# Last layer: GpSimd makes some of the shifted copies of VectorE's exponential, each issued beside a first step that reads PSUM; the planner's thresholds there set anew

## The chip, the cores and the metric

The kernel runs on one core of a Trainium2 chip. The core has five engines with instruction queues of their own: TensorE (PE; its weight loads are listed as PEld), VectorE (DVE), ScalarE (ACT), GpSimd (POOL) and SyncE (SP), which issues the DMAs. Each runs its queue in order, and they meet through semaphores. The metric is the device time of one execution in microseconds, as the median over runs.

## The reference

Four layers are added to a stream `x` of 2048 tokens by 512 features: A, B, A, B. Each normalizes its input, projects it to 32 heads of 16 features, attends, and projects back.

```python
# layer A (inside four segments of 512 tokens, causal, and a memory of the segments before)
logits = einsum(qs, ks) * scale + mask;  p = softmax(logits);  a_dot = p @ vs
a_mem = phi(qs) @ M / (phi(qs) @ z + 1e-06);  o = g * a_mem + (1 - g) * a_dot
M = M + phi(ks)^T @ vs;  z = z + sum(phi(ks))
# layer B (all 2048 tokens against all, no mask)
scores = einsum('bhqd,bhkd->bhqk', q, k) * Dh ** (-0.5)
o = einsum('bhqk,bhkd->bhqd', softmax(scores), v)
# x = x + A(ln(x)); x = x + B(ln(x)); x = x + A(ln(x)); x = x + B(ln(x))
```

A layer B needs 32 x 2048 x 2048 exponentials, 128 million, and a matmul on either side of them. The last layer is a B.

## The kernel before

**Tiles.** A head's scores are made in transposed blocks of 128 keys by 512 queries, one PSUM bank each (PSUM has 8 banks of 512 float32 columns). Heads are done in groups: one group is the heads of a 128-row chunk `c` with parity `e`, four heads at the row offsets 0, 32, 64, 96, against one segment of 512 queries. For such a group the queries are copied into a masked tile `qm` (line 1424). In layer 3 a group has up to 64 banks.

**Units.** The loop in `attention` takes unit after unit. A unit is two or three banks of scores: PE computes them (`qm` against keys `KB`), then one ACT instruction takes the exponential of all of them at once, from PSUM into the tile `pT` (line 1514, 128x1024 for two banks, 128x1536 for three). Two sets of three banks alternate, so PE fills one while ACT reads the other. Some units later PE multiplies `pT` with the values (17 columns: 16 features and a one for the sum) into an accumulator bank, four heads in four column quarters.

**The exponential on DVE.** A part of the banks goes another way, called `dx`. When `compose` finds room, a unit gives up its third bank (bank 2 or 4 of PSUM), or a spare bank is used, or both. DVE reads this bank in a first step (`dx_first`, line 1121): scale, add a constant and write as uint16, whose bits are those of a bfloat16 near the exponential. One bank makes a first step of 512 columns, two banks one of 1024. The bits alone are too rough, so the tile is shifted: `dx_shift` (line 1184) adds a small constant to the uint16 values, which makes another rough exponential with its error elsewhere, and so on in a chain of four (`EXP_D`), or of three with weighted values (`W_D`). Every member of the chain is multiplied with the values by PE and added up in the accumulator. A chain runs over one, two or four banks at once, so a shift is 512, 1024 or 2048 columns wide. It goes in place, or into another free space: the tiles `dxw`, and in the last layers tiles that are no longer needed, `KA`, `QA`, `VA`, `woA`, `phk`, `phq`, `KB`, `VB`, `xT`. In the profile shifts therefore read `xT<-phq`, `KB<-VB` and the like, and first steps `VB<-ps`.

**What sets the order.** Nothing is decided on the chip. A class `Sched` records each instruction with a planned end, from durations given with each call, and derives the semaphores from what is read and written. The `Builder` asks this plan what to issue next: a first step only if DVE's planned time is near enough to the start of the unit (`dx_room`); shifts when DVE has credit, or to fill the time until a bank is ready (`fill`); products of shifted tiles when their planned end has passed (`pv_some`). Thresholds of these questions are class constants, and the list `PIECES` sets them anew whenever ACT's planned time passes the next of some forty marks. Four chains (`CHAINS`) may be open at once, each a generator `task_dx`. `dx_now` holds the space and banks of an open chain, `dx_use` how many readers a space still has, `dxq` the products that wait to be issued.

GpSimd has three kinds of work: causal masks of layer A, ones in the values, and the query masks `qm` in layers B. SP issues loads, transposes and the output.

Of the kernel before, what the change touches and what calls it, by code (L numbers as in the profile page):

```python
# [5 lines left out]
ALU = mybir.AluOpType  # L6
# [3 lines left out]
D = 512  # L10
# [12 lines left out]
UNIT, DXB, ACC = (0, 4), 3, 7  # L23
# [55 lines left out]
class Sched:  # L79


    def __init__(self):
        self.ops = {e: [] for e in ENGS}
        self.t = {e: 0.0 for e in ENGS}
        self.tiles = []

        self.streams = []
# [7 lines left out]
    def estimate(self, op, ns, gap, tile):  # L95
# [17 lines left out]
        elif e == "sp":  # L113
            st = max(ready, self.t[e])
            self.t[e] = st + max(gap, 600)
            op.end = st + ns
        else:
# [5 lines left out]
    def add(self, eng, fn, reads=(), writes=(), deps=(), name="", banks=(), ns=300, gap=None, tile=None):  # L123
# [47 lines left out]
        self.estimate(op, ns, max(ns - 85, 60) if gap is None else gap, tile)  # L171
# [86 lines left out]
class Builder:  # L258
# [9 lines left out]
    DX_RES, CHAINS, ALT, ALTS, ALTA = 0, 4, 0, 3, (1, 1, 1, 1)  # L268
    ORDER = [[(-4.6, 7.7, 7.6, 0.9, -10), (3.8, -10.8, 0.4, 20, -10.8), (19, 59.6, 22, 59.8, 12), (31, 44.3, 46.9, 10.6, 0.2)],
             [(-1.5, -6.7, -5.8, 20.8, 1.2), (-5.2, -1.6, 28.5, 28, 7), (21, 35.0, 8.2, 30, 27.7), (21, 48.0, 37, 23.6, 12.2)]]  # L270
    PIECES = [(20.0, {'DXA_REST': 14, 'EVAC_ACT': -300, 'LOW': 32}),
              (60.0, {'AHEAD': 500, 'CR_W': 1900, 'DXA_REST': 10, 'EVAC_ACT': -300, 'LOW': 24, 'wide': True}),
              (100.0, {'AHEAD': 500, 'CR_W': 1900, 'DQ': 1900, 'EVAC_ACT': -300, 'wide': True}),
              (140.0, {'AHEAD': 300, 'CR_W': 1400, 'DQ': 2200, 'DX_T': 480, 'EVAC_ACT': 0}),
              (180.0, {'DMA_LATE': 300, 'DX_FIN': 2500, 'DX_T': 480, 'PE_B': 5, 'PE_LOW': 5}),
              (220.0, {'DMA_LATE': 600, 'DX_FIN': 2000, 'DX_T': 430, 'LOW': 16, 'PE_B': 4, 'PE_LOW': 6, 'PVN': 6}),
              (260.0, {'DX_RES': 2, 'HOR': 100, 'LOW': 24, 'NEAR_N': 200, 'PVN': 4}),
              (300.0, {'DX_RES': 2, 'HOR': 100, 'MARGIN': 700, 'NEAR_N': 200}),
              (340.0, {'DMA_LATE': 300, 'DQ': 1900, 'DX_RES': 2, 'FILLS': 1, 'HOR': 100, 'MARGIN': 700, 'NEAR_E': 80, 'NEAR_N': 200}),
              (380.0, {'DMA_LATE': 300, 'DMA_STEPS': 3, 'DQ': 2500, 'DX_RES': 2, 'DX_T': 330, 'FILLS': 1, 'HOR': 100, 'MARGIN': 700, 'NEAR_E': 0, 'NEAR_N': 200}),  # L280
              (420.0, {'DMA_LATE': 300, 'DMA_STEPS': 3, 'DQ': 2500, 'DX_RES': 2, 'DX_T': 330, 'FILLS': 1, 'HOR': 100, 'MARGIN': 700, 'NEAR': 6, 'NEAR_E': 0, 'NEAR_N': 200}),
# [1604 lines left out]
```

## Time and profile before

| | |
|---|---|
| median of 3 runs | 1772.88 us (1772.08 to 1774.62) |
| span of the profiled execution | 1772.3 us |
| ACT busy in it | 1729.2 us, 98% |
| DVE busy | 1521.1 us, 86% |
| PE busy | 1586.6 us, 90% |
| POOL busy | 287.2 us, 16% |

Busy time is the time in which at least one instruction of the engine ran; the rest is waiting. Line numbers are those of the kernel before. A group's row gives the line, engine, operation, output and input tile and shape, the count, then busy time in us and the mean of one in ns, and behind the second bar the idle time in front of them with what ended it. Because several lines are helpers (line 445 records every matmul), tiles tell more than lines. Two instructions that follow each other on DVE or ACT overlap a little in the record, the second starting before the first has ended.

### The profile page before, as it was taken

The numbers are of one execution on the slowest core, as the hardware profiler recorded it, in microseconds if no ns is written. First come the engines' busy times: TensorE is split into PE (matmuls) and PEld (weight loads), VectorE is DVE, ScalarE is ACT, GpSimd is POOL, SyncE is SP. The second block draws the span as 40 slices with busy tenths as digits, with TensorE's granted clock in tenths as the row PEclk, the third lists the DMA queues.
The fourth block names the chain that finished last, engine by engine and source line by source line (L and its number), as shares of the span: only waits on it lengthen the run. The fifth ranks groups of instructions, "written<-read, shape, count | busy, mean of one in ns | idle before, by whom it ended". The sixth has DMA issues, their size and how long they took to land.

```text
span 1772.3 us, 42500 instructions
## 1 busy us (share of the span) xinstructions
PE 1586.6 (90%) x17251; PEld 568.1 (32%) x17436; DVE 1521.1 (86%) x3001; ACT 1729.2 (98%) x1674; POOL 287.2 (16%) x656
## 2 busy tenths in 40 slices
PE   7889898889898989989989988988898898889988
PEld 4445454553224222233222332332222222222222
DVE  6677766589995999888999879768999999999997
ACT  7989998999999999999999999999999999999998
POOL 4622515110006000113000240141100000000000
PEclk9999998999999999999999999999999999999999
DMA  6021111000001000000000010110000000000000
GB/s 173 20 46 29 32 20 25 14 9 7 13 7 16 4 13 13 2 19 14 8 13 13 5 34 7 19 26 13 2 13 1 1 7 7 1 1 7 7 1 13
DMA packets 86180, 30.01 MB, mean 17 GB/s; under 512 B 78816, under 2 KB 85472, under 8 KB 85984
## 3 DMA queue, kind: packets, MB, share of 16 engines
q1 hardware_dynamic: 85984, 27.29, 7.6%
q8 instruction: 136, 2.23, 0.5%
q14 instruction: 60, 0.49, 0.1%
HBM read 6.30 MB, written 2.10 MB: 5 GB/s over the span
## 4 chain that ended last, share of the span: by engine, by line
ACT 52%; PE 22%; issue 17%; DVE 6%; POOL 2%; DMA 1%; SPq 0%; ACTq 0%; DVEq 0%; POOLq 0%
ACT pT L1514 51%; PE ps L445 22%; POOL pT L1529 2%; DVE QA L1121 1%; ACT amem L697 0%; DVE dxw L1184 0%; DVE dxw L1121 0%; DMA xT<-xn 0%; DVE rg L809 0%; DVE VB L1121 0%; DVE VB L480 0%; DVE KA L1646 0%; DVE VA L1184 0%; DVE ob L1628 0%; DVE phq L700 0%
## 5 line engine op out<-in xcount | busy, mean ns | idle before, releaser
L1514 ACT ACTIVATE pT<-ps 128x1024 bf16<-128x1024 f32 (+4 forms) x1623 | 1697.0, 1201 | 27.8 <-PE ps L445 21.0
L445 PE MATMUL ps<-qm,KB 32*128 32x512 bf16 x3584 | 517.8, 384 | 79.0 <-ACT pT L1514 67.3
L445 PE MATMUL ps<-pT,VB 128*17 128x512 bf16 x2221 | 377.7, 384 | 8.7 <-ACT pT L1514 3.7
L1529 POOL TENSOR_SCALAR_AFFINE_SELECT pT<-pT 128x256 bf16<-128x256 bf16 (+2 forms) x524 | 213.0, 418 | 548.4 <-ACT pT L1514 535.9
L445 PEld LDWEIGHTS ps<-qm,KB 32*128 32x128 bf16 x3584 | 131.6, 91 | 458.1 <-ACT pT L1514 355.1
L1424 POOL TENSOR_SCALAR qm<-QB,par 128x512 bf16<-128x512 bf16 x88 | 66.9, 763 | 848.7 <-PE ps L445 769.4
L445 PEld LDWEIGHTS ps<-pT,VB 128*17 128x17 bf16 x2221 | 88.1, 87 | 240.0 <-issue 202.5
L1121 DVE TENSOR_SCALAR dxw<-ps 128x512 uint16<-128x512 f32 (+1 forms) x212 | 145.4, 697 | 4.5 <-PE ps L445 3.6
L445 PE MATMUL ps<-qm,KA 32*128 32x384 bf16 (+3 forms) x1024 | 104.3, 307 | 26.0 <-ACT pT L1514 19.5
L1121 DVE TENSOR_SCALAR VA<-ps 128x512 uint16<-128x512 f32 (+1 forms) x172 | 121.4, 720 | 5.8 <-PE ps L445 4.7
L1184 DVE TENSOR_SCALAR dxw<-dxw 128x1024 uint16<-128x1024 uint16 (+1 forms) x302 | 121.0, 411 | 3.5 <-PE ps L445 1.7
L1121 DVE TENSOR_SCALAR QA<-ps 128x512 uint16<-128x512 f32 (+1 forms) x168 | 117.8, 716 | 4.9 <-PE ps L445 4.1
L445 PE MATMUL ps<-qm,QA 32*128 32x512 bf16 x512 | 103.6, 384 | 19.9 <-ACT pT L1514 18.6
L445 PE MATMUL ps<-VA,pT 128*128 128x51 bf16 (+1 forms) x2560 | 108.6, 188 | 14.1 <-POOL pT L1529 6.5
L445 PE MATMUL ps<-dxw,VW 128*17 128x512 bf16 x437 | 108.7, 381 | 0.2 <-DVE dxw L1184 0.2
L445 PEld LDWEIGHTS ps<-VA,pT 128*128 128x128 bf16 x2560 | 85.6, 97 | 63.8 <-POOL pT L1529 30.3
L1121 DVE TENSOR_SCALAR VB<-ps 128x512 uint16<-128x512 f32 (+1 forms) x117 | 92.1, 804 | 2.8 <-PE ps L445 2.1
L1121 DVE TENSOR_SCALAR KB<-ps 128x512 uint16<-128x512 f32 (+1 forms) x98 | 77.9, 808 | 2.5 <-PE ps L445 2.1
L445 PE MATMUL ps<-pT,VA 128*17 128x512 bf16 x386 | 76.7, 384 | 2.2 <-ACT pT L1514 1.8
L445 PE MATMUL ps<-dxw,VB 128*17 128x512 bf16 x256 | 74.1, 381 | 0.0
L445 PE MATMUL ps<-VB,pT 128*128 128x34 bf16 (+1 forms) x1788 | 69.4, 186 | 2.0 <-ACT pT L1514 1.1
L445 PE MATMUL ps<-xT,wB 128*128 128x512 bf16 x224 | 63.0, 393 | 5.8 <-issue 2.7
(292 smaller groups left out, 2408.1 us busy)
## 6 DMA issues: line engine op xcount, KB each, us to landing
out_dram<-x SPq DMA_DIRECT2D x8, 256.0 KB, 2.1
x<-in_A_x_dram SPq DMA_DIRECT2D x3, 512.0 KB, 5.1
wB<-in_B_wqkv_dram SPq DMA_DIRECT2D x1, 1536.0 KB, 11.7
xT<-xn SPq DMA_TRANSPOSE x60, 2.4
oT<-ob SPq DMA_TRANSPOSE x36, 2.4
x<-in_A_x_dram SPq DMA_DIRECT2D x4, 128.0 KB, 2.7
wA<-in_A_wq_dram SPq DMA_DIRECT2D x1, 512.0 KB, 5.1
wA<-in_A_wk_dram SPq DMA_DIRECT2D x1, 512.0 KB, 6.1
```

The lines of the kernel that those rows point to most:

```text
L445: self.sc.add("pe", lambda e: e.matmul(out, lhsT, rhs, start=start, stop=stop, skip_group_check=True), reads=reads, banks=[(bank, "w", all ...
L1121: self.sc.add("dve", lambda e: e.tensor_scalar(d, o, SCALE * LOG2E * 128, W_C if dxs[0][:3] in self.wt else EXP_C, op0=ALU.mult, op1=ALU.add),
L1184: self.op("dve", lambda e: e.tensor_scalar(o, w, d, None, op0=ALU.add), reads=self.b_dxw[b0][:len(ents)], writes=wr, ns=(295, 425, 560, 69 ...
L1424: self.op(eng, (lambda m, q, col: lambda e: e.tensor_scalar(m, q, col, 0.0, op0=ALU.mult, op1=ALU.add))(m, q, col), reads=[bq, self.b_par] ...
L1514: self.sc.add("act", (lambda dst, src: lambda e: e.activation(dst, src, ACT.Exp, scale=SCALE))(dst, src), writes=self.b_pT[slot * 3 + i:sl ...
L1529: self.op("pool", (lambda blk, pat: lambda e: e.affine_select(blk, blk, pattern=pat, compare_op=ALU.is_ge, fill=0.0, base=0, channel_multi ...
```

## The change

The class constant `PSH` switches the new part on. `PIECES` sets it to 2 at 1240 us of ACT's planned time, which is in the last layer, and `PSH_N` is 12, from 1720 us on 20. The rest of the new `PIECES` holds differences only, where the old one repeated values, and before 1240 it gives the same thresholds: both programs are identical up to there. From 1240 on the thresholds differ as well.

With `PSH` on, `dx_first` looks behind every first step whether GpSimd's planned time is early enough. If so, `pool_claim` picks an open chain whose next member can be made (or opens a waiting one), and `pool_part` issues a copy of as many banks as the first step has on GpSimd: the same addition of a constant on uint16. It waits for the DVE instruction in front of the first step (`self.sc.ops["dve"][-2]`), beside the semaphores that its data need. A shift of four banks thus becomes two to four copies. A claimed chain goes on when all its copies have been issued; what is left is issued at once in `task_dx`. In the plan, GpSimd and those DVE instructions that do not touch PSUM now exclude each other (`shared`).

```diff
+    def shared(self, eng, at, ns):
+        for e, a, b in self.held:
+            if e != eng and a <= at < b:
+                at = b
+        self.held = self.held[-5:] + [(eng, at, at + ns)]
+        return at
...
+        elif port and self.lock:
+            st = self.shared(e, max(self.t[e], ready), gap)
+            op.end = self.t[e] = max(st + gap, ready + ns)
...
+    PSH, PSH_N, DXP = 0, 12, 0
...
+              (1240.0, {'NEAR': 14, 'PVN': 3, 'PVHOLE': 250, 'DMA_LATE': 300, 'PSH': 2}),
+              (1280.0, {'NEAR': 10, 'DMA_LATE': 600}),
...
+              (1640.0, {'FILL_DVE': 0, 'DX_T': 480, 'DXA': 4, 'DX_WAIT': 200}),
...
+        if self.PSH and self.wide and max(self.sc.t["pool"], 0) <= self.sc.t["dve"] - (520, 1040)[k - 1]:
+            if not any(p and p["at"] < len(p["ents"]) for p in self.pooled):
+                self.pool_claim()
+            for p in self.pooled:
+                if p and p["at"] < len(p["ents"]):
+                    self.pool_part(p, k, self.sc.ops["dve"][-2])
+                    break
...
+    def pool_take(self, k, now):
+
+        b0, ents = now
+        g = ents[0][0]
+        j = self.dx_at[k] + 1 if self.dx_now[k] else 1
+        D = self.chords(ents)
+        if g is not self.cur and g not in self.sel or len(g.banks) - g.pos < self.PSH_N:
+            return False
+        b = b0 if self.dx_free(b0, len(ents)) or not self.dx_left(len(ents)) else self.dx_pick(len(ents))
...
+    def pool_part(self, job, n, sync):
+
+        b0, b, ents, i0 = job["b0"], job["b"], job["ents"], job["at"]
+        n = min(n, len(ents) - i0)
+        lo, hi = 512 * i0, 512 * (i0 + n)
+        w, o, d = self.dx_space(b0)[:, lo:hi], self.dx_space(b)[:, lo:hi], job["d"]
+        wr = [x for i in range(i0, i0 + n) for x in self.dx_writes(b, i)]
+        self.sc.add("pool", lambda e: e.tensor_scalar(o, w, d, None, op0=ALU.add), reads=self.b_dxw[b0][i0:i0 + n], writes=wr,
+                    deps=[sync] if sync is not None else [], ns=180 + 512 * n, gap=170 + 512 * n, name="dxp%d" % n)
```

What this does to the order, at three places. In the changed kernel lines have other numbers: 1134 is the first step, 1211 the shift, 1597 the exponential on ACT, 1507 the query mask, 1259 the new copy.

GpSimd's queue at the start of the last layer, before: the query masks and the ones in the values, and nothing more to the end.

```order
L1424 TENSOR_SCALAR qm<-QB,par 128x512 x4
L882 MEMSET VB 128x32 x3
L1424 TENSOR_SCALAR qm<-QB,par 128x512 x2
L882 MEMSET VB 128x32
L1424 TENSOR_SCALAR qm<-QB,par 128x512 x32
```

The same place of GpSimd's queue in the changed kernel:

```order
L1507 TENSOR_SCALAR qm<-QB,par 128x512 x6
L1259 TENSOR_SCALAR dxw<-dxw 128x512 x2
L1259 TENSOR_SCALAR QA<-dxw 128x512
L1507 TENSOR_SCALAR qm<-QB,par 128x512 x2
L1259 TENSOR_SCALAR QA<-dxw 128x512
L1259 TENSOR_SCALAR dxw<-phk 128x1024
L1507 TENSOR_SCALAR qm<-QB,par 128x512 x2
L1259 TENSOR_SCALAR dxw<-xT 128x512 x2
L1259 TENSOR_SCALAR woA<-KB 128x512 x2
L1259 TENSOR_SCALAR woA<-KB 128x1024
```

Copies now stand between the query masks: 200 of 512 and 54 of 1024 columns to the end of the program, with 26 masks among or behind them.

DVE's queue in the last layer behind the finish of the eighteenth group from the end (`x<-x,ps` adds the output projection to the stream), before:

```order
L1121 TENSOR_SCALAR VA<-ps 128x512 x2
L1184 TENSOR_SCALAR VB<-VB 128x2048
L1184 TENSOR_SCALAR VB<-VA 128x2048
L1184 TENSOR_SCALAR QA<-VB 128x2048
L1121 TENSOR_SCALAR KB<-ps 128x512
L911 TENSOR_TENSOR x<-x,ps 128x512
L1121 TENSOR_SCALAR KB<-ps 128x512 x2
L1184 TENSOR_SCALAR woA<-VB 128x2048
```

And in the changed kernel:

```order
L1134 TENSOR_SCALAR KA<-ps 128x512 x2
L1211 TENSOR_SCALAR xT<-KA 128x2048
L1134 TENSOR_SCALAR VB<-ps 128x512 x2
L924 TENSOR_TENSOR x<-x,ps 128x512
L1211 TENSOR_SCALAR VA<-xT 128x2048
L1134 TENSOR_SCALAR VB<-ps 128x512 x3
L1211 TENSOR_SCALAR QA<-VB 128x2048
L1134 TENSOR_SCALAR VB<-ps 128x512 x3
L1211 TENSOR_SCALAR phq<-VB 128x2048
```

More first steps stand between two shifts: where four shifts followed five first steps, four now follow ten.

ACT's queue where the two programs part (units of two and of three banks), before:

```order
L1514 ACTIVATE pT<-ps 128x1536 x4
L1514 ACTIVATE pT<-ps 128x1024 x2
L1514 ACTIVATE pT<-ps 128x1536 x3
L1514 ACTIVATE pT<-ps 128x1024
L1514 ACTIVATE pT<-ps 128x1536
```

And in the changed kernel:

```order
L1597 ACTIVATE pT<-ps 128x1536
L1597 ACTIVATE pT<-ps 128x1024
L1597 ACTIVATE pT<-ps 128x1536 x2
L1597 ACTIVATE pT<-ps 128x1024
L1597 ACTIVATE pT<-ps 128x1536
```

Units of two banks come in between sooner: of the eleven units before, eight have three banks; of the six that the second fence shows, four have.

140 lines of the change are left out of this document (91 added, 49 removed).

## The prediction

> **What bounds the kernel now.** I read the busy table of the page first, then the busy time by stage, cut where the order changes and after the last exponential, then the exponentials by shape, the waits of that stage, and single moments of the timeline. The place where the two programs part is found by laying the order beside DVE's timeline: the first DVE row that differs is this pair of shifts, of which the changed kernel keeps one at this place (start, us, instruction).
>
> ```profile
> 1251.61 0.75 DVE L1184 TENSOR_SCALAR dxw<-dxw 128x1024 uint16<-128x1024 uint16 x2
> ```
>
> ```profile
> PE 1586.6 (90%) x17251; PEld 568.1 (32%) x17436; DVE 1521.1 (86%) x3001; ACT 1729.2 (98%) x1674; POOL 287.2 (16%) x656
> ```
>
> ```profile
> 1252.00:1764.90 512.90, 460.87 (x4236) 116.61 (x4254) 494.34 (x782) 511.34 (x468) 19.35 (x25) 1.00 0.01 4
> 1764.90:1772.30 7.40, 3.20 (x14) 0.93 (x14) 3.83 (x10) 1.22 (x3) 0.00 (x0) 0.92 0.21 71
> ```
>
> The columns of the second view are the stretch, its length, then busy time and instructions of PE, PEld, DVE, ACT, POOL, the granted clock, DMA share and GB/s. All the time that the change can touch is the 512.9 us of the first row: before it both programs are the same, instruction for instruction, and the last five exponentials of three banks, with the output work of 7.4 us behind them, are the same too. In that stretch ACT is busy 511.34 us of 512.9: it bounds. DVE is next with 494.34, so 18.6 us of DVE are idle. PE has 52 us of idle; GpSimd is nearly empty. The clock is 1.00.
>
> ```profile
> L1514 ACT ACTIVATE pT<-ps 128x1024 bf16<-128x1024 f32 x278 | 286.2, 1127 | 0.9 <-PE ps L445 0.8
> L1514 ACT ACTIVATE pT<-ps 128x1536 bf16<-128x1536 f32 x190 | 285.4, 1548 | 0.6 <-PE ps L445 0.4
> ```
>
> ACT waited only 1.5 us in all there. So the stretch is as long as ACT has exponentials, as long as nobody makes it wait.
>
> ```profile
> PEld ps L445 <- ACT pT L1514: 219.6, 401, 1.0
> PEld ps L445 <- issue: 123.9, 491, 0.4
> PE ps L445 <- ACT pT L1514: 43.2, 129, 0.6
> POOL qm L1424 <- DVE woA L1184: 20.1, 1, 20.1
> ```
>
> These waits (total us, times, longest) say the same from the other side: PE stands behind ACT. No row of that list has anyone waiting for GpSimd.
>
> **The exponentials.** Counted in the order, both programs run 465 units from the parting on, but 20 of them have two banks where they had three: 277 and 188 become 297 and 168. The DVE exponential takes the 20 banks over. One such unit is 1548 - 1127 = 421 ns shorter, 20 of them 8.4 us. This is on the path that sets the end: **-8.4 us**, if ACT stays fed.
>
> **DVE.** It gets 48 more first steps of one bank, 14 fewer of two, 59 fewer shifts of 2048, 18 fewer of 1024 and 4 more of 512. Consecutive instructions overlap, so I price by the distance of starts, not by the durations:
>
> ```profile
> 1756.77 1.22 DVE L1121 TENSOR_SCALAR KB<-ps 128x1024 uint16<-128x1024 f32 x1
> 1757.90 0.68 DVE L1184 TENSOR_SCALAR KB<-KB 128x2048 uint16<-128x2048 uint16 x1
> 1758.50 0.68 DVE L1184 TENSOR_SCALAR KA<-KA 128x2048 uint16<-128x2048 uint16 x1
> 1759.10 0.42 DVE L1184 TENSOR_SCALAR xT<-xT 128x1024 uint16<-128x1024 uint16 x1
> 1759.44 0.42 DVE L1184 TENSOR_SCALAR KB<-KB 128x1024 uint16<-128x1024 uint16 x1
> ```
>
> A first step of two banks takes 1757.90 - 1756.77 = 1.13 us, a shift of 2048 0.60, one of 1024 0.34, so by the same slope about 0.21 for 512. A first step of one bank takes 0.61 (1663.33 to 1663.94, below). The sum: -59 x 0.60 - 18 x 0.34 + 4 x 0.21 + 48 x 0.61 - 14 x 1.13 = -35.4 - 6.1 + 0.8 + 29.3 - 15.8 = **-27.2 us** of DVE work. DVE isn't the bound, so this buys nothing itself; it is the cover for what follows.
>
> **GpSimd.** 254 copies are new, 200 of 512 and 54 of 1024. The one row of a GpSimd TENSOR_SCALAR in the stretch is the query mask (2-byte in and out, like the copies):
>
> ```profile
> L1424 POOL TENSOR_SCALAR qm<-QB,par 128x512 bf16<-128x512 bf16 x25 | 19.3, 774 | 417.4 <-PE ps L445 377.4 <-DVE woA L1184 20.1 <-DVE KB L1184 19.9
> ```
>
> Undisturbed it takes 0.69 (rows below), with its waits for DVE 0.77 on average. A copy of 1024 is not in the trace; it lies between 0.69 (if all were fixed cost) and 1.38 (if none were). How GpSimd's time grows with the width shows in the causal masks of the earlier layers:
>
> ```profile
> L1529 POOL TENSOR_SCALAR_AFFINE_SELECT pT<-pT 128x384 bf16<-128x384 bf16 x152 | 82.5, 544 | 165.0 <-ACT pT L1514 161.5
> L1529 POOL TENSOR_SCALAR_AFFINE_SELECT pT<-pT 128x128 bf16<-128x128 bf16 x176 | 54.1, 308 | 221.0 <-ACT pT L1514 217.2
> ```
>
> 256 more elements cost 0.236, so 512 more 0.47, and I take 0.69 + 0.47, rounded to 1.2. 200 x 0.77 + 54 x 1.2 = 219 us of 513: GpSimd has room, also at 1.38. Behind a copy stand 26 query masks in its queue. Each may come 0.7 to 1.4 us later; PE released most of the earlier ones, about 16 us of GpSimd idle before each (377.4 over 23), and nobody waited for one, so I cost that at nothing.
>
> **The price of sharing.** GpSimd and DVE do hold each other up here. Three moments:
>
> ```profile
> 1602.48 0.69 POOL L1424 TENSOR_SCALAR qm<-QB,par 128x512 bf16<-128x512 bf16 x1 [18.97 <-PE ps L445]
> 1602.58 1.14 DVE L1184 TENSOR_SCALAR KB<-VB 128x2048 uint16<-128x2048 uint16 x1
> ```
>
> ```profile
> 1663.45 0.69 POOL L1424 TENSOR_SCALAR qm<-QB,par 128x512 bf16<-128x512 bf16 x1 [20.12 <-DVE woA L1184]
> ```
>
> ```profile
> 1662.72 0.69 DVE L1184 TENSOR_SCALAR woA<-xT 128x2048 uint16<-128x2048 uint16 x1
> 1663.33 0.69 DVE L1121 TENSOR_SCALAR VB<-ps 128x512 uint16<-128x512 f32 x1
> 1663.94 0.49 DVE L1184 TENSOR_SCALAR KB<-KB 128x1024 uint16<-128x1024 uint16 x1
> ```
>
> In the first a shift begins 0.10 us into a GpSimd instruction and takes 1.14 instead of 0.68: 0.46 lost. It ends 0.55 behind GpSimd's end, so a shift can spend its first 0.13 us while GpSimd is still at work. The other two fences are the changed kernel in small: GpSimd is released by the DVE instruction in front of a first step (0.04 us after its end at 1663.41), runs beside the first step, which reads PSUM and takes its usual 0.69, and hangs over by 0.20 into the next shift, which takes 0.49 instead of 0.42: 0.07 lost. In the order 81 of the 254 copies have a shift right behind their first step; the others have another PSUM read or a finish there. Lower bound of the loss: nothing. By the near row 81 x 0.07 = 5.7 us. Upper bound, every copy meeting a shift as badly as the worst row: 254 x 0.46 = 117 us. I take 6, since the issue beside the first step makes each moment like the near row. Then DVE is 27.2 - 6 = 21 us lighter than before and stays covered by ACT: **0 us** on the path. The cover is gone at a loss of 27 us, 0.11 per copy.
>
> The Trainium skill (SBUF — State Buffer, section "Who interferes with whom") says that whichever of the two engines starts first keeps the shared ports for its whole instruction and that the other one blocks fully. The row at 1602.58 agrees but for the 0.13 us; by the rule alone the 81 shifts would lose the whole 0.20 each, 16 us, still under the cover.
>
> **PE and the rest.** PE gets 40 more matmuls of 17 columns (a DVE bank needs three or four of them, an ACT bank one) and 9 fewer fills. Each is between nothing, when it runs beside three others in another column quarter, and 0.22 us, the distance of starts within one quarter (1763.11, 1763.33, 1763.55):
>
> ```profile
> 1763.11 0.38 PE L445 MATMUL ps<-dxw,wA 128*17 128x512 bf16 x1
> 1763.33 0.38 PE L445 MATMUL ps<-KB,wA 128*17 128x512 bf16 x1
> 1763.55 0.38 PE L445 MATMUL ps<-dxw,wA 128*17 128x512 bf16 x1
> ```
>
> That is 0 to 8.8 us of PE, against 52 idle. A PE instruction that waits for a copy holds the scores behind it, and so ACT. I take a rise of ACT's waits from 1.5 to 2.5 us, **+1.0**; the ends are 0 and what an earlier stretch shows, 4 us lost in 440, so 4.7 in 504, a rise of 3.2:
>
> ```profile
> 450.00:890.00 440.00, 398.89 (x3921) 127.59 (x3967) 390.68 (x793) 435.97 (x443) 60.52 (x150) 1.00 0.06 11
> ```
>
>  The SP queue is the same. A DVE shift that reads a copy's result stands at least two instructions behind it, in 70 of 76 cases more than four, so GpSimd's end is past: nothing.
>
> Sum on the profiled execution: 1772.3 - 8.4 + 1.0 = 1764.9. The median of the runs, 1772.88, lies 0.6 above that span, so 1765.5 for the median of the changed kernel.
>
> **Rivals.** *The ports take back what they free (slower).* If a copy on GpSimd costs DVE as much as the shift that it replaces, the shifts' 40.7 us come back as longer shifts, 0.16 per copy, between the two rows (0.07 and 0.46), and the first steps' 13.5 us come on top. DVE's own idle can take some: it waited for PE in 26 places, in 13 rows of the waits that sum to 8.8 us, here the first and the last.
>
> ```profile
> DVE VB L1121 <- PE ps L445: 1.5, 6, 0.5
> ...
> DVE KB L1184 <- PE ps L445: 0.2, 1, 0.2
> ```
>
> If all of these vanish, DVE ends 13.5 - 8.8 = 4.7 us late, if none, 13.5: 1777 to 1786. It decides at 0.11 to 0.12 per copy. For it: 0.46 was measured, and a copy that waits for PE to finish with its target, or for the copy in front, starts late in its first step and hangs over by more than 0.20. Against: only 81 shifts stand next. The Trainium skill speaks for it (Perfetto Trace Analysis, "Optimizing Scalar/DVE Operations"): moving work between these two might not help, as they share a port.
>
> *The gain goes into waits of ACT (no change).* The DVE banks come bunched: the order has long runs of two-bank units soon after the parting. A two-bank unit gives PE only about 1.0 us, with a first step's scores and the added 17-column matmuls to fit in. Where PE led before, from 1200 to 1240 us, ACT was busy 38.6 of 40:
>
> ```profile
> 1200.00:1240.00 40.00, 36.17 (x274) 10.30 (x278) 32.89 (x67) 38.58 (x35) 5.37 (x7) 1.00 0.09 14
> ```
>
> At half that loss, 1.8%, over the stretch, ACT waits 9 us, and the time is 1772. Against: PE's 43 us behind ACT.
>
> *The change does nothing:* excluded, the order has 254 copies on GpSimd and 20 banks off ACT.
>
> **How the numbers follow.** My forecast 0.68, its own range 1762 (no waits at all: 8.5 and 1.5 off, rounded) to 1768.5 (4.7 us of waits, and the spread of the runs); no change 0.13; slower 0.19. A difference of 0.2%, 3.5 us, is about what a measurement can tell from none. The range reaches from 1761.5 over the no-change case to 1776 and leaves out the slower one. The chances are those of the cases.
>
> **What the profile will show.** Right: ACT's exponentials of three banks down by 20, ACT busy over 99% from 1252 us to the last exponential, now near 1757.5; copies of 512 near 0.69 to 0.8; shifts of 2048 with a mean under 0.72; DVE at about 93 to 96% of the stretch. Wrong by the ports: shifts with a mean over 0.85, DVE without idle, PE waiting for first steps. Wrong by PE: ACT idle of 5 us or more, ended by PE, with PE rows that wait for GpSimd. What would break the forecast first is a copy on uint16 that takes far longer than the mask's 0.69.

## The result, and the profile after

The changed kernel is slower: 1830.86 us in the median of 4 runs (1829.09 to 1833.79), against 1772.48 (1770.21 to 1774.62) of the kernel before in the same comparison. The ratio is 1.033, 95% interval 1.0307 to 1.0351. The forecast was 1765.5, and the range ended at 1776.

The profiled execution has a span of 1827.7 us, 55.4 more than before. The first part of its page, and the busy time by stage, with the same columns as in the prediction:

```profile
PE 1646.2 (90%) x17467; PEld 569.3 (31%) x17467; DVE 1531.0 (84%) x2962; ACT 1731.0 (95%) x1674; POOL 759.1 (42%) x910
```

```profile
1252.00:1820.00 568.00, 492.53 (x4271) 117.63 (x4268) 502.90 (x740) 510.35 (x466) 487.05 (x276) 0.95 0.01 4
```

All of it lies in the last layer: the stretch to the last exponential took 568.0 us where it took 512.9. ACT's work there is no longer than before (510.35, before 511.34). What is new is that ACT is idle for 57.6 us of it, before 1.6. And GpSimd, which was to be busy for 219 us beside 19 of query masks, is busy for 487. The exponentials by shape and the waits of the stage say who is late:

```profile
L1597 ACT ACTIVATE pT<-ps 128x1024 bf16<-128x1024 f32 x297 | 295.2, 1051 | 39.4 <-PE ps L458 38.8
L1597 ACT ACTIVATE pT<-ps 128x1536 bf16<-128x1536 f32 x169 | 245.7, 1470 | 18.2 <-PE ps L458 17.3
```

```profile
ACT pT L1597 <- PE ps L458: 56.1, 74, 4.5
PEld ps L458 <- ACT pT L1597: 150.5, 305, 1.1
PEld ps L458 <- POOL VB L1259: 12.6, 9, 2.7
```

The units did go from three banks to two (169 of three where there were 190). But ACT waits for PE in 74 places, up to 4.5 us, and PE waits for copies, of which no row before spoke. Summed over all tiles, the view of the copies' line lists these waiters:

```profile
PEld ps L458: 51.1, 35
PE ps L458: 38.0, 30
```

(A weight load and its matmul wait in the same place, so the two rows largely tell the same time twice.) And this is why the results are late: the copies of one pair of tiles in the stretch, by shape (behind the count: busy time in us, mean of one in ns), with the query masks:

```profile
L1259 POOL TENSOR_SCALAR woA<-KB 128x512 uint16<-128x512 uint16 x12 | 18.9, 1596 | 6.1 <-DVE dxw L1211 5.4 <-DVE KB L1211 0.6
L1259 POOL TENSOR_SCALAR woA<-KB 128x1024 uint16<-128x1024 uint16 x4 | 11.1, 2766 | 1.7 <-PE ps L458 0.9 <-DVE KB L1211 0.7 <-POOL woA L1259 0.2
L1507 POOL TENSOR_SCALAR qm<-QB,par 128x512 bf16<-128x512 bf16 x25 | 19.3, 781 | 1.6 <-PE ps L458 1.6
```

A copy of 512 takes 1.6 us and one of 1024 takes 2.8, where the sum had 0.77 and 1.2. Over all tiles (197 copies of 512, 54 of 1024 in the trace) the means are 1.62 and 2.86, together 474 us. One stall in the timeline shows the chain from GpSimd to ACT:

```profile
1541.84 5.93 POOL L1259 TENSOR_SCALAR QA<-VB 128x1024 uint16<-128x1024 uint16 x2
1547.82 0.39 PE L458 MATMUL ps<-QA,VW 128*17 128x512 bf16 x1 [3.46 <-POOL QA L1259]
1548.14 0.39 PE L458 MATMUL ps<-qm,KB 32*128 32x512 bf16 x3
1548.61 0.69 DVE L1134 TENSOR_SCALAR KB<-ps 128x512 uint16<-128x512 f32 x1 [2.03 <-PE ps L458]
1548.63 1.02 ACT L1597 ACTIVATE pT<-ps 128x1024 bf16<-128x1024 f32 x1 [2.79 <-PE ps L458]
1549.15 0.61 PE L458 MATMUL ps<-qm,QA 32*128 32x512 bf16 x2
1549.87 1.45 ACT L1597 ACTIVATE pT<-ps 128x1536 bf16<-128x1536 f32 x1 [0.21 <-PE ps L458]
```

Two copies of 1024 stand in a row on GpSimd. A product of one of them waits on PE for 3.46 us; behind it in PE's queue stand the three score matmuls of the next unit, which have nothing to do with the copy; and only when they have run can both DVE's next first step and ACT's next exponential begin, the latter after 2.79 us of idle time.

The last two rows show that the stall has a tail. The score matmuls take 0.61 us there where they took 0.39 at 1548.14. The granted clock, the third number from the end, has fallen in between:

```profile
1547.00:1548.00 1.00, 0.18 (x3) 0.09 (x3) 0.00 (x0) 0.00 (x0) 1.00 (x2) 1.00 0.00 0
1549.00:1550.00 1.00, 1.00 (x6) 0.13 (x4) 0.30 (x1) 0.79 (x2) 1.00 (x2) 0.50 0.00 0
```

It stays at 0.50 to 1552 us; in that time PE is never idle, and ACT waits for it again, 0.21 us at 1549.87 and 0.47 at 1551.79. A fall to 0.50 also comes in or right behind the stalls around 1291, 1509 and 1570 us, in each of which PE runs nothing for at least 1 us. But one at 1375 us comes although PE was busy for at least 0.40 of each of the ten microseconds before. What makes the clock fall is therefore not shown.

The third place where time went is DVE. Summed over the rows by shape, its shifts of 2048 have a mean of 0.829 us (145 of them; before 0.687, 204) and those of 1024 a mean of 0.570 (48; before 0.419, 68). That is 145 x 0.142 + 48 x 0.151 = 28 us of DVE, 0.11 per copy: the whole relief of 27 us that the fewer shifts were to give.

### The profile page after: what moved, and what is told of

It is laid out like the page before. It is cut to its first block, busy times and chain, and to the rows that moved or that the text cites. A ratio compares the mean times of both kernels' runs of the same rounds, so it can differ in the third digit from the quotient of the medians.

```text
span 1827.7 us, 43147 instructions
## 1 busy us (share of the span) xinstructions
PE 1646.2 (90%) x17467; PEld 569.3 (31%) x17467; DVE 1531.0 (84%) x2962; ACT 1731.0 (95%) x1674; POOL 759.1 (42%) x910
## 4 chain that ended last, share of the span: by engine, by line
ACT 36%; PE 25%; issue 15%; DVE 13%; POOL 10%; DMA 1%; POOLq 0%; SPq 0%; ACTq 0%; DVEq 0%
ACT pT L1597 36%; PE ps L458 25%; POOL xT L1259 2%; POOL KB L1259 2%; POOL pT L1612 2%; DVE KB L1134 1%; POOL VB L1259 1%; DVE VB L1134 1%; POOL QA L1259 1%; DVE dxw L1211 1%; POOL woA L1259 1%; DVE xT L1211 1%; DVE KA L1730 1%; DVE KA L1134 1%; POOL phq L1259 1%
## 5 line engine op out<-in xcount | busy, mean ns | idle before, releaser
L458 PE MATMUL ps<-qm,KB 32*128 32x512 bf16 x3584 | 529.3, 391 | 64.4 <-ACT pT L1597 45.9
L1211 DVE TENSOR_SCALAR dxw<-dxw 128x1024 uint16<-128x1024 uint16 (+1 forms) x309 | 128.4, 426 | 3.6 <-PE ps L458 1.5
L458 PE MATMUL ps<-qm,QA 32*128 32x512 bf16 x512 | 109.5, 395 | 13.3 <-ACT pT L1597 11.1
L1134 DVE TENSOR_SCALAR KB<-ps 128x512 uint16<-128x512 f32 (+1 forms) x116 | 89.2, 784 | 24.3 <-PE ps L458 23.7
L458 PE MATMUL ps<-xT,wA 128*128 128x512 bf16 (+1 forms) x276 | 77.2, 386 | 1.3 <-DVE xT L671 0.9
L458 PE MATMUL ps<-QA,VW 128*17 128x512 bf16 x308 | 70.9, 386 | 5.3 <-POOL QA L1259 5.3
```

Of the source, the lines that this page charges most:

```text
L458: self.sc.add("pe", lambda e: e.matmul(out, lhsT, rhs, start=start, stop=stop, skip_group_check=True), reads=reads, banks=[(bank, "w", all ...
L1134: self.sc.add("dve", lambda e: e.tensor_scalar(d, o, SCALE * LOG2E * 128, W_C if dxs[0][:3] in self.wt else EXP_C, op0=ALU.mult, op1=ALU.add),
L1211: self.op("dve", lambda e: e.tensor_scalar(o, w, d, None, op0=ALU.add), reads=self.b_dxw[b0][:len(ents)], writes=wr, ns=(295, 425, 560, 69 ...
```

## The experiments

Two things had to be told apart: why a copy takes 1.48 us at the least where the query mask takes 0.69, and, once that is known, which of the copies' length, their place and the new thresholds made the kernel slower.

### What makes a copy long

The copy differs from the query mask in two ways: its type is uint16 and not bfloat16, and it has one operation (an addition) where the mask has two (a multiplication by a column in SBUF and an addition of 0.0). The theory after the result was the type; the rival was the form. The first probe is the kernel before, with instructions at the head of GpSimd's queue, four of each kind one behind the other on tiles not yet in use:

```diff
+        A, B, C = self.dxw[:, 0, 0:512], self.dxw[:, 1, 0:512], self.dxw[:, 2, 0:512]
+        W, Z = self.dxw[:, 0, 0:1024], self.dxw[:, 1, 0:1024]
+        probe(lambda e: e.tensor_scalar(B, A, 22.0, None, op0=ALU.add))
+        probe(lambda e: e.tensor_scalar(Z, W, 22.0, None, op0=ALU.add))
+        probe(lambda e: e.tensor_scalar(B, A, 1.0, 22.0, op0=ALU.mult, op1=ALU.add))
+        probe(lambda e: e.tensor_scalar(B.bitcast(bf), A.bitcast(bf), 22.0, None, op0=ALU.add))
...
```

> The kernel before, with GpSimd instructions put at the head of its queue, four of each form, on a scratch tile, while nobody else uses it; the order of all other instructions is that of the kernel before. Theory 'type' (GpSimd is slow on uint16 elements, whoever else is at work): the addition of 512 uint16 takes 1.48 us as in the changed kernel, 1024 take 2.76, a second operation changes little, and the same on bfloat16 takes about 0.69. Theory 'form' (one operation with an immediate is slow, the mask's two operations are fast): uint16 with two operations near 0.69, bfloat16 with one operation near 1.48. Theory 'ports' (VectorE holds the copies up): all forms near 0.69 here. If uint16 only on one side (in or out) is slow, the two mixed forms tell which. A 32-bit integer addition of 256 packed pairs should take 0.55 to 0.9 us if a two-input element costs about twice a one-input one; if over 1.48 there is nothing to gain from it. The whole kernel: later than before by about the probes' 45 us or less.

The timeline of GpSimd in it (start, time of four together):

```profile
5.90 6.26 POOL L550 TENSOR_SCALAR dxw<-dxw 128x512 uint16<-128x512 uint16 x4
12.25 11.32 POOL L551 TENSOR_SCALAR dxw<-dxw 128x1024 uint16<-128x1024 uint16 x4
23.65 2.72 POOL L552 TENSOR_SCALAR dxw<-dxw 128x512 uint16<-128x512 uint16 x4
26.45 6.20 POOL L553 TENSOR_SCALAR dxw<-dxw 128x512 bf16<-128x512 bf16 x4
```

The lone addition takes 6.26 / 4 = 1.57 us on uint16 and 1.55 on bfloat16, so the type is not the cause. Nor is it DVE, as the third theory in the expectation had it: while the bfloat16 row runs, from 26.4 to 32.7 us, DVE has no instruction at all. The same addition behind a multiplication by 1.0, on uint16, takes 0.68. The type was also tried in the changed kernel itself, whose copies were made to read and write through a bfloat16 view:

```diff
-        w, o, d = self.dx_space(b0)[:, lo:hi], self.dx_space(b)[:, lo:hi], job["d"]
+        w, o, d = self.dx_space(b0)[:, lo:hi].bitcast(dt.bfloat16), self.dx_space(b)[:, lo:hi].bitcast(dt.bfloat16), job["d"]
```

> The changed kernel, every instruction in the same place, but the copies on GpSimd read and write the same bytes as bfloat16 instead of uint16, so they add the constant to the value and not to its bits: the shifted exponentials of GpSimd are not those of the reference. Theory 'type': copies take 0.69 and 1.2 us, nobody waits for GpSimd, and the time is what was predicted with fast copies, 1762 to 1769 (ratio 0.994 to 0.998). Theories 'form' and 'ports': copies stay at 1.48 and 2.76 and the time at 1825 to 1835. Theory 'thresholds' (the new order is bad by itself): copies are fast but the time stays above 1800.

It took 1831.14 us, ratio 1.033 (1.0305 to 1.0356), like the changed kernel. The view of the copies' line (durations least/median/longest, in ns) shows them as long as ever:

```profile
L1259 POOL TENSOR_SCALAR woA<-KB x16: 1482/1554/2768, 1275.6 to 1453.1; 128x512 bf16<-128x512 bf16 x12, 128x1024 bf16<-128x1024 bf16 x4
```

So the theory of the type fell. A second probe of the same kind asked what of the form it is: two operations of any kind, the pair of a multiplication with an addition, or a scalar from SBUF.

```diff
+        probe(lambda e: e.tensor_scalar(B, A, 1.0, 22.0, op0=ALU.mult, op1=ALU.add))
+        probe(lambda e: e.tensor_scalar(Z, W, 1.0, 22.0, op0=ALU.mult, op1=ALU.add))
...
+        probe(lambda e: e.tensor_scalar(B, A, 22.0, 0.0, op0=ALU.add, op1=ALU.add))
+        probe(lambda e: e.tensor_scalar(B, A, 22.0, 1.0, op0=ALU.add, op1=ALU.mult))
+        probe(lambda e: e.tensor_scalar(B, A, 1.0, None, op0=ALU.mult))
...
+        probe(lambda e: e.tensor_scalar(B, A, self.hmask[:, 0:1], None, op0=ALU.add))
```

> The kernel before with GpSimd instructions on a scratch tile at the head of its queue, as in the first probe. If the count of operations decides: multiply-add, add-add and add-multiply all take 0.68 for 512 uint16, a lone multiplication and a lone addition of a scalar from SBUF 1.48. If the multiplication in front decides: add-add and add-multiply are slow, a lone multiplication fast. If the scalar's kind decides: the lone addition from SBUF is fast. Multiply-add of 1024 uint16 takes 1.15 to 1.25, of 256 0.42 to 0.46, on bfloat16 0.69. The whole kernel: about as the probes' length, 25 to 30 us, later than before.

The rows stand in the order of the diff; between L551 and L553, and between L555 and L558, others are left out:

```profile
5.90 2.73 POOL L550 TENSOR_SCALAR dxw<-dxw 128x512 uint16<-128x512 uint16 x4
8.71 4.42 POOL L551 TENSOR_SCALAR dxw<-dxw 128x1024 uint16<-128x1024 uint16 x4
...
15.16 7.94 POOL L553 TENSOR_SCALAR dxw<-dxw 128x512 uint16<-128x512 uint16 x4
23.18 2.72 POOL L554 TENSOR_SCALAR dxw<-dxw 128x512 uint16<-128x512 uint16 x4
25.98 6.25 POOL L555 TENSOR_SCALAR dxw<-dxw 128x512 uint16<-128x512 uint16 x4
...
38.87 6.53 POOL L558 TENSOR_SCALAR dxw<-dxw,hmask 128x512 uint16<-128x512 uint16 x4
```

Multiplication then addition takes 0.68 for 512 columns and 1.10 for 1024, addition then multiplication 0.68. Two additions take 1.98, a multiplication alone 1.56, an addition with a scalar from SBUF 1.63. So neither the number of operations nor the kind of scalar decides: of the forms tried, the pair of one multiplication and one addition is the one that is fast, in either order. None of the three outcomes that the expectation named came as it stood. (The two whole kernels took 1826.88 and 1804.17 us, a single run each, the first 54 us more than the kernel before where 45 or less was expected; only the probes' own rows are used here.)

### The changed kernel with the fast form

The copy's result stays the same if the value is multiplied by 1.0 first. This kernel is the changed one, with the same order of instructions on every engine; only the form of the copy differs:

```diff
-        self.sc.add("pool", lambda e: e.tensor_scalar(o, w, d, None, op0=ALU.add), reads=self.b_dxw[b0][i0:i0 + n], writes=wr,
+        self.sc.add("pool", lambda e: e.tensor_scalar(o, w, 1.0, d, op0=ALU.mult, op1=ALU.add), reads=self.b_dxw[b0][i0:i0 + n], writes=wr,
```

> The changed kernel, every instruction in the same place, with one edit: a copy multiplies by 1.0 and adds the constant (two operations, as the query mask has) instead of adding alone; the result is the same. Theory 'form' (GpSimd runs the one-operation instruction at 2.5 ns per element and the two-operation one at 1): copies take 0.68 and about 1.2 us, shifts of 2048 on VectorE a mean of 0.69 to 0.72, ScalarE's idle from 1252 us to the last exponential stays under 5 us, and the time is what was predicted for fast copies, 1762 to 1769 (ratio 0.994 to 0.998). Rival 'ports': the copies are fast, but shifts still lose 0.11 us per copy or more, and the time is 1772 to 1790. Rival 'late copies by plan': PE waits for GpSimd 20 us or more although the copies are fast, 1775 or more.

It took 1767.49 us (1761.21 to 1771.27, 12 runs) against 1773.61 of the kernel before: 0.9965, interval 0.995 to 0.9979. It is faster than both kernels, than the one before by only 6 us. Its span is 1767.0, and the stretch, the exponentials and the only row of its waits in which PE stands behind a copy:

```profile
1252.00:1759.50 507.50, 465.56 (x4296) 113.46 (x4290) 475.67 (x745) 504.04 (x470) 199.49 (x278) 1.00 0.01 4
```

```profile
L1597 ACT ACTIVATE pT<-ps 128x1024 bf16<-128x1024 f32 x298 | 304.1, 1116 | 2.1 <-PE ps L458 2.0
L1597 ACT ACTIVATE pT<-ps 128x1536 bf16<-128x1536 f32 x171 | 259.3, 1541 | 1.3 <-PE ps L458 1.3
```

```profile
PEld ps L458 <- POOL QA L1259: 0.3, 1, 0.3
```

ACT is idle for 3.5 us. PE, with the same instructions, is busy for 465.56 us at a clock of 1.00, where the changed kernel had 492.53 at 0.95; 465.56 / 0.95 is 490, so by this estimate nearly all of these 27 us of PE come from the clock. The shifts have their old length, 0.695 (145 of 2048) and 0.439 (50 of 1024): 145 x 0.008 + 50 x 0.020 = 2.2 us of DVE lost to 254 copies, 0.01 per copy. How the two kernels come apart is seen at one place. Here a copy of 512 begins beside a first step in each; first the changed kernel, its copies and the shift that DVE makes meanwhile:

```profile
1318.90 4.87 POOL L1259 TENSOR_SCALAR woA<-KB 128x512 uint16<-128x512 uint16 x3 [0.63 <-DVE KB L1211]
1320.57 0.94 DVE L1211 TENSOR_SCALAR QA<-KB 128x2048 uint16<-128x2048 uint16 x1
```

Then the same copies and the same shift with the fast form:

```profile
1318.54 0.62 POOL L1259 TENSOR_SCALAR woA<-KB 128x512 uint16<-128x512 uint16 x1 [1.43 <-DVE KB L1211]
1319.73 0.62 POOL L1259 TENSOR_SCALAR woA<-KB 128x512 uint16<-128x512 uint16 x1 [0.58 <-DVE KB L1134]
1320.20 0.70 DVE L1211 TENSOR_SCALAR QA<-KB 128x2048 uint16<-128x2048 uint16 x1
1320.98 0.62 POOL L1259 TENSOR_SCALAR woA<-KB 128x512 uint16<-128x512 uint16 x1 [0.63 <-DVE QA L1211]
```

A copy of 0.62 is over about when the first step is, so each is released anew beside the next one, and DVE's shift takes 0.70. A copy of 1.5 us reaches over two DVE instructions; the next copies no longer wait for their place but for the copy in front, and the shift takes 0.94. With nothing but the form of 254 instructions changed, the span went from 1827.7 to 1767.0, by 60.7 us: the whole loss of 55.4 hangs on it.

### The thresholds and the copies, one without the other

The new thresholds without copies (`PSH` left out of `PIECES`):

```diff
-              (1240.0, {'NEAR': 14, 'PVN': 3, 'PVHOLE': 250, 'DMA_LATE': 300, 'PSH': 2}),
+              (1240.0, {'NEAR': 14, 'PVN': 3, 'PVHOLE': 250, 'DMA_LATE': 300}),
```

> The changed kernel with the copies switched off, the new thresholds kept; no instruction of GpSimd is added. By its order it has 12 units fewer of three banks and 18 more of two than before, about 1 us more of ScalarE's work. Theory 'late copies' (the loss is PE waiting for slow copies): 1770 to 1785, since the thresholds were set for another order but nothing waits for GpSimd. Theory 'thresholds': above 1800.

1781.55 us, 1.0052 (1.0035 to 1.0068). The copies with the old thresholds are the other half: `PIECES` as before, with `'PSH': 2` at 1240 and `'PSH_N': 20` at 1720 added, in the changed kernel's slow form of the copy and in the fast one.

> The changed kernel with the thresholds of the kernel before: 184 copies of 512 and 56 of 1024 on GpSimd. Theory 'late copies': 1815 to 1845, ScalarE idle 50 us or more in the last layer. Theory 'thresholds': 1760 to 1775.

> The thresholds of the kernel before with copies of two operations (184 of 512, 56 of 1024). By its order ScalarE has 6 units of three banks and 1 of two fewer than before, about 9.5 us less work. Theory 'form', with the copies covered: 1762 to 1770. If the new thresholds are what makes fast copies pay: 1770 to 1785.

With the lone addition 1834.76 us, 1.0355 (1.0322 to 1.0388, 2 runs); with multiplication and addition 1781.34, 1.0047 (1.0028 to 1.0066). So the loss does not need the new thresholds: with the old ones the lone additions cost as much. And the gain of the fast form needs both parts: thresholds alone lose 0.5%, fast copies alone lose 0.5%, together they win 0.35%. Why each of the two loses alone stays open.

### What long copies cost with nobody waiting for them

To see the ports' part without late results, additions were put into the kernel before that no instruction reads: beside first steps chosen like those of the change, a lone addition from a tile that is no longer used to another one (`amem` to `ob`), released by the DVE instruction in front of the first step. The first attempt planned the additions with the changed kernel's durations:

```diff
+        if self.wide and self.PSH and self.ncopy < 254 and self.pool_at <= self.sc.t["dve"] - (520, 1040)[k - 1]:
+            self.idle_copy(k, self.sc.ops["dve"][-2])
...
+        op = Op("pool", len(pl), lambda e: e.tensor_scalar(o, w, 22.0, None, op0=ALU.add), "idle%d" % n)
...
+        self.pool_at = max(self.pool_at, sync.end + 60) + 170 + 512 * n
```

> The kernel before, with 254 one-operation uint16 additions on GpSimd in the last layer (171 of 512, 83 of 1024, released like the copies, by the VectorE instruction in front of a first step) on two tiles that are dead by then; nobody waits for them, and every other engine has the order of the kernel before. It shows what slow GpSimd work costs through the shared ports alone. Theory 'late copies' (most of the loss is PE waiting for copies' results): shifts of 2048 grow from 0.69 to 0.8 to 0.85, some 35 to 45 us on VectorE, of which its idle takes half, so 1785 to 1800. Rival 'ports are the whole loss': 1820 or more. Rival 'ports cost nothing': 1770 to 1776.

1885.19 us, 1.0643 (1.0619 to 1.0666): more than the change itself, and in the range of the rival that the ports are the whole loss. But it doesn't show the ports alone. GpSimd's queue grew so long that the query masks behind the additions came late, as these waits show:

```profile
PE ps L445 <- POOL qm L1450: 56.1, 10, 11.3
PEld ps L445 <- POOL qm L1450: 31.0, 5, 9.0
```

The attempt was made again with the additions spaced by their measured time, of which 102 of 512 and 73 of 1024 then found a place:

```diff
-        self.pool_at = max(self.pool_at, sync.end + 60) + 170 + 512 * n
+        self.pool_at = max(self.pool_at + 150, sync.end + 60) + 360 + 1280 * n
```

> As the run with 254 idle additions, but they are spaced by their true length, so that GpSimd's queue never piles up and the query masks come in time: 102 of 512 and 73 of 1024, one operation each, 365 us of GpSimd, nobody waits for them, all other engines in the order of the kernel before. Theory 'late copies': PE does not wait for GpSimd; shifts lose 0.12 to 0.22 us per addition, 21 to 39 us of VectorE, less the 9 us in which VectorE waited for PE anyway, so 1784 to 1803. If the ports cost nothing on the path: 1770 to 1776. If they are the whole loss of the change: 1820 or more.

1790.83 us, 1.0105 (1.0079 to 1.0131), and the profile has no wait of PE for GpSimd:

```profile
1252.00:1780.70 528.70, 473.05 (x4212) 121.70 (x4228) 517.38 (x776) 515.38 (x465) 389.42 (x197) 1.00 0.01 4
```

The stretch is 15.8 us longer. DVE, with the same work as before, is busy 23.0 us longer (517.38, before 494.34), because shifts of 2048 now take 0.795 in the mean (204) and those of 1024 0.510 (64); its idle time fell from 18.6 to 11.3, and the difference is the 15.8. So 175 long additions hold DVE up by about 204 x 0.108 + 64 x 0.091 = 28 us, 0.16 each, with nobody waiting for what they write. The way to ACT leads over PE again: summed over the rows of its waits, PE stands 21.6 us behind DVE, before 2.0. The time lies in the range of the first theory: for these 175 additions the ports cost a part of the change's loss, not the whole.

The last run of this kind gave the changed kernel's plan the measured durations of the lone addition, so that products of copies are not issued before the copies are there:

```diff
-                    deps=[sync] if sync is not None else [], ns=180 + 512 * n, gap=170 + 512 * n, name="dxp%d" % n)
+                    deps=[sync] if sync is not None else [], ns=202 + 1280 * n, gap=192 + 1280 * n, name="dxp%d" % n)
```

> The changed kernel with the one-operation copies as they are, but the plan reckons with their measured time, 1.48 and 2.76 us instead of 0.69 and 1.20; it then issues 102 copies of 512 and 60 of 1024. Theory 'late copies' (the loss comes from a plan that takes results too early): PE waits for GpSimd under 10 us in all, and the time is 1775 to 1790. Rival 'ports' (slow copies cost VectorE's shifts as much as they free, wherever they are planned): PE hardly waits for GpSimd, but shifts of 2048 take 0.8 us or more in the mean and the time is 1800 to 1825.

1801.94 us, 1.0171 (1.014 to 1.0202, 2 runs), with 162 copies:

```profile
1252.00:1792.40 540.40, 463.99 (x4180) 119.19 (x4213) 465.16 (x670) 523.55 (x470) 340.84 (x186) 0.99 0.01 4
```

```profile
PEld ps L458 <- POOL xT L1259: 1.6, 3, 0.7
```

The late results are all but gone; the row is the largest wait of PE for a copy in it. That takes half of the loss away. What stays is 12 us more of exponentials on ACT (523.55, before 511.34), since the plan now leaves more banks to ACT (204 units of three, before 190), and 15.3 us more of ACT's idle time, behind PE, which stands 21.8 us behind DVE (before 2.0). The shifts of 2048 have a mean of 0.780 (140). So neither theory came alone: PE hardly waits for a copy, but the time is in the range of the rival, and the shifts are just short of its 0.8. Planning honestly with a slow copy does not make it pay.

### What the place of a copy is worth

The other half of the change's idea is that a copy is issued beside a first step, which reads PSUM. Two kernels keep the fast form and the order of every queue, and change only what a copy waits for: in one the first step itself, so that it runs beside the instruction behind it; in the other its data alone.

```diff
+        d0 = [x for x in [q.last_write for q in rd + wr] + [r for q in wr for r in q.reads.values()] if x is not None and x.eng == "dve" and not x.is_dma]
+        if sync is not None:
+            d0.append(self.sc.ops["dve"][-1])
...
+        op.deps = [x for x in op.deps if x.is_dma or x.eng != "dve"] + sorted(d0, key=lambda x: x.idx)[-1:]
```

(In the second, the two lines with `sync` are left out.)

> The kernel with multiply-and-add copies (median 1767.5, 0.9965 of before), in the same order; only the place of a copy is changed: it waits for the first step itself and not for the DVE instruction in front of it, so it runs beside the instruction behind the first step. 81 of 254 copies have a shift there. If GpSimd then holds the shift up (the row of the prediction: 0.46 lost by a shift that begins early in a GpSimd instruction, 0.13 of which it can use), each of the 81 loses about 0.49 beside a copy of 0.62 and 0.92 beside one of 1.05, some 47 us in all, more than DVE's 32 us of idle: shifts of 2048 with a mean near 0.95, time 1775 to 1790. If the shift, which begins before the semaphore has reached GpSimd, holds GpSimd up instead: shifts under 0.73, copies of 512 with a mean over 0.75, time 1766 to 1773. If the place of a copy does not matter: shifts 0.70, copies 0.62, time 1766 to 1769.

> The same kernel with multiply-and-add copies in the same order, but a copy waits for its data alone and not for the DVE instruction in front of a first step: it begins as soon as GpSimd and its data are there. If the place beside a first step is what keeps the ports' price low, copies that begin at any moment meet more shifts: by chance 200 shifts in 507 us, each begun within the 0.49 or 0.92 us of a copy in which it has to wait, half of that lost, 0.05 us per copy of 512 and 0.17 per copy of 1024, 18 us in all, half of DVE's idle: shifts of 2048 with a mean near 0.77, time 1767 to 1774. If the place is worth nothing: shifts 0.70 and 1766 to 1769.

One instruction later costs 0.8%: 1781.75 us, 1.0048 (1.0028 to 1.0069). With no place given, no gain is left in the median: 1770.53, 0.9999 (0.9982 to 1.0016). But this second result is weak. The ten runs go from 1766.74 to 1778.08, the interval only just misses that of the kernel with the place (to 0.9979), and the profiled execution has a span of 1766.5, as short as the other's 1767.0, with shifts of 2048 at 0.716 (145) and not the 0.77 that was expected. Whether the place is worth anything against none stays open. The stretch of the first, and of its waits the one of ACT and the largest of PE for a copy:

```profile
1252.00:1770.00 518.00, 471.94 (x4273) 117.49 (x4271) 490.43 (x740) 504.79 (x466) 223.82 (x277) 1.00 0.01 4
```

```profile
ACT pT L1605 <- PE ps L458: 12.4, 30, 1.2
PEld ps L458 <- POOL VB L1263: 4.3, 6, 1.3
```

Its shifts have means of 0.780 (145) and 0.536 (48), 17 us more of DVE than in the kernel with the copies in their place. That is much less than the 47 us of the first expectation, because the copies pay as well: 0.731 in the mean for 512 (197), not 0.62. So neither of the two expected outcomes came alone: sometimes the copy holds the shift, sometimes the shift the copy. Two moments of its timeline, the shift first and the copy first:

```profile
1326.11 0.68 DVE L1211 TENSOR_SCALAR xT<-KA 128x2048 uint16<-128x2048 uint16 x1
1326.34 0.92 POOL L1263 TENSOR_SCALAR VA<-phq 128x512 uint16<-128x512 uint16 x1 [1.29 <-DVE VB L1134]
1332.55 1.04 POOL L1263 TENSOR_SCALAR VB<-xT 128x1024 uint16<-128x1024 uint16 x1 [2.44 <-DVE QA L1134]
1332.90 0.97 DVE L1211 TENSOR_SCALAR dxw<-QA 128x1024 uint16<-128x1024 uint16 x1
```

The copy that begins in a shift takes 0.92 where it takes 0.62 undisturbed; the shift that begins in a copy takes 0.97 where it takes 0.42. The Trainium skill (SBUF — State Buffer, section "Who interferes with whom") states, for DVE instructions in a two-port mode, that the engine which began first keeps the shared ports for its whole instruction. These rows agree but for a short start: the copy ends 0.47 us behind the shift's end, the shift 0.28 behind the copy's, so 0.15 and 0.14 us of them were done before.

## Why the prediction was wrong

**The step that failed** is the price of a copy, "200 x 0.77 + 54 x 1.2 = 219 us". It was taken from the query mask as the one GpSimd TENSOR_SCALAR of the stretch, with "2-byte in and out, like the copies" as what makes them alike. The likeness that counted was another one: the mask multiplies and adds, the copy only adds. The trace of before had no lone addition on GpSimd, and the bounds for 512 columns were not taken from both sides, as they were for 1024: the mask's time stood as the copy's time, with no upper end. Measured, it is 1.62 and 2.86, 474 us. The last sentence of the forecast named this case, "a copy on uint16 that takes far longer than the mask's 0.69", but gave it no chance and no time in the range, and it suspected the type.

**What followed from it**, step by step:

- *ACT, -8.4 us.* Held: 21 fewer exponentials of three banks in the changed kernel. In the kernel with the fast form, ACT's busy time in the stretch fell by 7.3 us.
- *PE waits for a copy, +1.0 (0 to 3.2).* In the changed kernel ACT's idle time rose by 56 us instead, behind PE, which waited for copies and ran at a lower clock behind some of these waits. With the fast form it rose by 1.9. The mechanism stood in the forecast ("a PE instruction that waits for a copy holds the scores behind it, and so ACT"); its size hung on the copy's length.
- *The price of sharing, 6 us, cover gone at 0.11 per copy.* In the changed kernel 28 us, 0.11 per copy, just at that point; with the fast form 2.2 us, 0.01 per copy, less than forecast, as a copy of 0.62 ends about with the first step beside it. The 16 us that the prediction worked out from the Trainium skill's rule (SBUF — State Buffer, section "Who interferes with whom") would have been further off.
- *The rival of the ports.* It expected shifts over 0.85, DVE without idle, and 1777 to 1786. The shifts came to 0.829, but DVE was idle for 65 us of the 568: DVE's total did not set the end. What did is the other sign that was named, ACT idle behind PE "with PE rows that wait for GpSimd". The sentence of the Trainium skill (Perfetto Trace Analysis, "Optimizing Scalar/DVE Operations") that moving work between DVE and GpSimd might not help holds for the lone addition (28 us back, of 27 us that DVE was to be relieved by) and not for the pair (2.2 of 27).
- *GpSimd has room.* With copies of 0.62 and 1.05 it is busy for 199 us, somewhat less than the 219 + 19 of the sum. With the lone addition 487 of 568 us, and then its queue is itself a reason for late results.

With the price right, the rest of the sum would have done: the kernel with the fast form has a span of 1767.0 where the sum had 1764.9, and a median of 1767.49, inside the forecast's own range of 1762 to 1768.5. (A slip without weight: the 4 us lost in 440 are 4.6 in 504, not 4.7.)

How the 55 us divide between late results and the ports could not be settled cleanly. Late results were taken away by the plan with true durations, which also changed the order; ports were shown alone on the order before. A kernel with results that are late without GpSimd holding the ports was not found. The waits of PE, summed over their rows in the stretch, give the order of size: in the changed kernel PE stands 38.0 us behind copies and 15.9 behind DVE, before 0 and 2.0, with the fast form 0 and 3.2. Late results are the larger part, and the slower DVE reaches ACT over PE too.

Open is also the part of the TensorE clock: it was granted at 0.95 in the stretch of the changed kernel and at 0.99 to 1.00 in the stretches of the four kernels shown whose copies or additions did not stall PE for long. It made the loss longer, since ACT stood idle behind a PE that was busy without a pause at 0.50. How much of the 55 us that is was not tested; PE was busy 27 us longer, and only a part of that need have reached ACT.

## What to carry to other kernels

Price an operation that moves to another engine from a row of the same engine with the same operations in it; a row with the same engine, name and width but another pair of operations can be off by more than a factor of two, and without such a row the range has to take in an upper end. On GpSimd, write a scaling or an added constant as a multiplication and an addition in one instruction, even if one of them does nothing (measured here on 16-bit values, 256 to 1024 columns). When an in-order engine gets work whose result another in-order engine consumes, a late result costs everything that stands behind the consumer in its queue, so look there first, before counting busy time.

## What the runs showed of the hardware

- GpSimd's tensor_scalar on 128x512: multiplication with addition 0.62 (in the kernel) to 0.68 us, a lone addition 1.48 at the least in the kernel and 1.57 in the probe, a lone multiplication 1.56, two additions 1.98. On 128x1024 the pair takes 1.05 to 1.10, the lone addition 2.76 at the least. uint16 and bfloat16 are alike.
- An addition of packed pairs as int32, 256 columns of two tensors, takes 0.78 us (3.12 for four), so a two-tensor addition of the same bytes is twice as quick as the lone addition of a scalar:

```profile
56.69 3.12 POOL L557 TENSOR_TENSOR dxw<-dxw 128x256 int32<-128x256 int32 x4
```

- What GpSimd costs DVE depends on the length and the place of its instructions more than on how many there are: 254 short copies beside first steps cost DVE 0.01 us each, the same copies one instruction later 17 us in all on top, 175 long additions 0.16 us each.
- In the changed kernel TensorE was granted half the clock in and behind several stalls of PE; the score matmuls took 0.61 us at 0.50 and 0.39 at 1.00.
